# Sinks staged in other buffers, and transposes and products with the values placed later in TensorE's written order: a banded attention with a gated MLP

## Chip, cores, metric

One Trainium2 chip, one core. The metric is the device time of one execution in microseconds (us), the median of several runs. Engines: PE is TensorE (PEld its weight loads), DVE is VectorE, ACT is ScalarE, POOL is GpSimd, SP is SyncE, which issues all DMAs here.

## What is computed

Attention over 4 batches, 8 heads, 768 positions of 64 dimensions; a query sees the first `n_sink` = 4 keys (the sinks) and the last `window` = 128 keys. The result, with the heads side by side (512 columns), goes through an MLP with a short convolution as its gate:

```
scores = scale * q @ k.T           # kept where key < 4 or 0 <= query - key < 128
a   = softmax(scores);  x = a @ v  # x: batch, position, 512
h   = relu(x @ w_in)               # 1024 columns
g   = sigmoid(3-tap convolution of h along the positions)
out = (h * g) @ w_out              # 512 columns
```

All in float32. To keep float32's precision in fast products, most operands are split into a high part and a low part (names with H and L), and three products replace one.

## The kernel before

`banded(c)` (L390) is the path that runs here. Heads are taken in pairs ("groups"): 4 pairs per batch, 16 in all. A pair has 6 tiles of 128 queries, so it takes 6 **steps**; the whole attention has 96 steps, `NSTB` = 24 per batch. Batch 0 (steps 0 to 23) uses plain float32 products and runs beside the loading of the MLP's weights; from batch 1 on keys and queries are split (`A.prep`, L252 to L298).

**What a step does.** The main loop runs over `i`. It writes down, for step `i` and two earlier steps, the parts of the work; each pass has three **slots**, and after each slot come pieces of the MLP (`fill`) and pieces of preparation (`todo`):

- slot 0: `scores(g, t)` (L484) for step `i`: four products into PSUM tiles "sc" (L334, L335), masks and row minimum on DVE (L509, L510), exp on ACT (L513), sum and reciprocal on DVE (L515, L516), normalisation on POOL (L518).
- slot 1: `transp(g, t)` (L527) for step `i - D1` = `i - 1`: two transposes of the weights on PE into "pts" (L548), a copy to SBUF tile "pT" on ACT (L550), two selects on POOL (L552, L554). At every third tile (`u == 2`) the four sink columns of three tiles are gathered: high parts on ACT (L560), low parts on DVE (L561), one transpose of 72 columns on PE (L562, tile "tk"), a copy "sT" on ACT (L564).
- slot 2: `pv(g, t)` (L566) for step `i - D2` = `i - 2`, when a pair's last tile is through: products of the values with pT (L580), five products of the sinks' values `vsr` with sT (L598), and `A.xout`, which splits the result into xH on ACT (L342) and xL on DVE (L343). At a batch's last pair the MLP's next pieces begin here (`cuts`).

The MLP of a batch is spread over the next batch's steps: a unit is 12 products for h (L184, 258 or 260 columns), a chain ACT, DVE, POOL (L191 to L202), and 6 products for the output (L211, 512 columns) in PSUM tiles "po". When 8 units are added up, `second` (L204) copies po to a tile "stm" with tag "st" on ACT (L215) and SP writes it out (L216). "st" has three buffers. The last batch's MLP has no attention beside it.

The preparation of a pair transposes its raw keys and queries in four pieces (`turn_k(0)`, `turn_k(1)`, `turn_q(0)`, `turn_q(1)`): three transposes on PE (L287, L262), two copies on ACT (L290, L250), two subtractions on DVE (L293, L269); after the second piece two DMAs kk<-kk on SP (L297, L298). `coming(n)` says when the pieces are due, as distances in steps. Each piece frees one of four raw buffers, and `fetch()` then issues the next load (L351).

PSUM tag "T" has two buffers. The preparation's transposes, the sinks' transpose and the results px of `pv` (two at a time from batch 1 on) all take theirs from it.

`sink_split` (L376) loads the first four rows of a batch's values to `raw`, splits them to `hi` (ACT, L380) and `lo` (DVE, L381), and issues 18 DMAs that place them in `vsr` (L387). `vsr` exists once. The three tiles have tag "st". The weights come through three buffers of tag "nat" (L97, L100) and are loaded up to step 18.

**What sets the order.** From `i` = `PINNED` = 26 on, PE runs its instructions exactly in the order in which the loop writes them (`c.pin`). Before that, and on all other engines and queues throughout, a planner orders the instructions by its own costs and by their place in the program; each engine then runs its list in order and waits where an operand or a buffer isn't ready.

```
for i in range(NST + D2):
    ...
    for slot in range(SLOTS):
        if slot == 0 and i < NST:
            scores(g, t)
        if slot == 1 and 0 <= i - D1 < NST:
            transp(*steps[i - D1][1:])
        if slot == 2 and 0 <= i - D2 < NST:
            pv(*steps[i - D2][1:])
            ...
        acc += rate / SLOTS
        while acc >= 1.0 and fill:
            fill.pop(0)()
            acc -= 1.0
        while todo and i + (slot + 1) / SLOTS >= todo[0][0]:
            todo.pop(0)[1]()
```

Of the kernel before, what the change touches and what calls it, by code (L numbers as in the profile page):

```python
# [10 lines left out]
F32 = mybir.dt.float32  # L11
F32R = mybir.dt.float32r
# [5 lines left out]
P = 128  # L18
D = 64
NEG = 1.0e9  # L20
NS = 4
SP = 16
SR = 6 * NS
# [15 lines left out]
def f(ap):  # L39
    return ap.bitcast(F32)  # L40
# [334 lines left out]

def sink_split(c, m, vsr, b):  # L376

    raw, hi, lo = (m.mp.tile([P, 512], d, tag="st", name=f"sink{n}{b}", bufs=3)[0:NS] for d, n in ((F32, "r"), (F32R, "h"), (F32R, "l")))
    c.nc.sync.dma_start(raw.rearrange("s (h d) -> s h d", d=D), c.v[b].rearrange("h s d -> s h d")[0:NS])
    c.nc.scalar.copy(hi, raw)  # L380
    c.nc.vector.tensor_tensor(out=lo, in0=raw, in1=f(hi), op=ALU.subtract)  # L381
    for u in range(3):
        for part, val in enumerate((hi, hi, lo)):
            for j in range(2):
                r = SR * part + 2 * NS * u + NS * j
                dst, src = (f(x).rearrange("s (g j d) -> s g j d", j=2, d=D)[:, :, j] for x in (vsr[r:r + NS, u], val))
                c.nc.sync.dma_start(dst, src)  # L387


def banded(c):  # L390

    nc = c.nc
    m = Moe(c)
    A = Attn(c, m.x, KW, m.mp, m.ps)
    T = A.T
    NPAIR = c.H // 2
    NG = c.B * NPAIR
    cp = c.es.enter_context(c.tc.tile_pool(name="bc", bufs=1))
    ap, ps = A.ap, A.ps
# [34 lines left out]
    n0, n1 = T * KW, 3 * NPAIR * P  # L434
# [92 lines left out]
    def transp(g, t):  # L527
        s = st[g]
        hf, u = divmod(t, 3)
        if g < NPAIR:  # L530
            parts = 1 + (t > 0)
            for w in range(parts):
                for j in range(2):
                    c.pin(nc.tensor.transpose(pts[:, w, j, :], s.pe[hf][:, u, j, 0:P] if w else s.pe[hf][:, u, j, KW:SW], c.ident))
            s.pT[t] = ap.tile([P, 2, 2, P], F32, tag="pT", name=f"pT{g}_{t}", bufs=PTB)
            nc.scalar.copy(s.pT[t][:, 0:parts], pts[:, 0:parts])
            if u == 2:
                pk = m.ps.tile([P, P], F32, tag="T", name=f"tk{g}_{t}", bufs=2)
                sk = ap.tile([P, 6, SP], F32, tag="sk", name=f"sk{g}_{hf}")
                nc.scalar.copy(sk, s.pe[hf].rearrange("p t h k -> p (t h) k")[:, :, P:P + SP])  # L540
                c.pin(nc.tensor.transpose(pk[0:6 * SP, :], sk.rearrange("p t k -> p (t k)"), c.ident))
                s.sT[hf] = ap.tile([6 * SP, P], F32, tag="sT", name=f"sT{g}_{hf}")
                nc.scalar.copy(s.sT[hf], pk[0:6 * SP, :])
            return
        pt = pts[:, A.n % 2]
        A.n += 1
        for j in range(2):
            c.pin(nc.tensor.transpose(pt[:, j, :], s.pe[hf][:, u, j, NS:KW], c.ident))  # L548
        own = keytile(g, t)[:, :, 0]
        nc.scalar.copy(own, pt)  # L550
        if t:
            nc.gpsimd.affine_select(out=keytile(g, t - 1)[:, :, 1], in_=own, pattern=[[0, 2], [-1, P]],  # L552
                                    compare_op=ALU.is_gt, fill=c.zero, base=0, channel_multiplier=1)
            nc.gpsimd.affine_select(out=own, in_=own, pattern=[[0, 2], [1, P]], compare_op=ALU.is_ge, fill=c.zero,  # L554
                                    base=0, channel_multiplier=-1)
        if u == 2:
            pk = m.ps.tile([P, P], F32R, tag="T", name=f"tk{g}_{t}", bufs=2)
            sinks = s.pe[hf].rearrange("p t h k -> p (t h) k")[:, :, 0:NS]
            sk = ap.tile([P, 3, 6, NS], F32R, tag="sk", name=f"sk{g}_{hf}")
            nc.scalar.copy(sk[:, 0:3:2], sinks.rearrange("p (o t) k -> p o t k", o=1).to_broadcast([P, 2, 6, NS]))  # L560
            nc.vector.tensor_tensor(out=sk[:, 1], in0=sinks, in1=f(sk[:, 0]), op=ALU.subtract)  # L561
            c.pin(nc.tensor.transpose(pk[0:3 * SR, :], sk.rearrange("p a t k -> p (a t k)"), c.identr))  # L562
            s.sT[hf] = ap.tile([3 * SR, P], F32R, tag="sT", name=f"sT{g}_{hf}")
            nc.scalar.copy(s.sT[hf], f(pk[0:3 * SR, :]))  # L564

    def pv(g, t):  # L566

        s = st[g]
        hp = g % NPAIR
        hf, u = divmod(t, 3)  # L570
        if u < 2 or (g >= NPAIR and hf == 0):
            return
        halves = [hf] if g < NPAIR else [1, 0]
        px = {h: m.ps.tile([P, 3, P], F32, tag="T", name=f"px{g}_{h}", bufs=2).rearrange("p t k -> p (t k)") for h in halves}
        open_ = set()

        def product(j, kt, qt, pT):
            h, at = divmod(qt, 3)
            n = pT.shape[-1]
            c.pin(nc.tensor.matmul(px[h][D * j:D * j + D, P * at:P * at + n], s.v[:, kt, j, :], pT, start=(h not in open_), stop=False,  # L580
                                   skip_group_check=True))

        if g < NPAIR:
            for t1 in range(t, 3 * hf - 1, -1):
                for w in range(1 + (t1 > 0)):
                    for j in range(2):
                        product(j, t1 - w, t1, s.pT[t1][:, w, j, :])
                    open_.add(hf)
        else:
            for kt in range(T - 1, -1, -1):  # L590
                pT = s.pT.pop(kt).rearrange("p h a k -> p h (a k)")
                for lo, hi in [(0, 2 * P)] if kt % 3 < 2 else ([(P, 2 * P)] if kt < T - 1 else []) + [(0, P)]:
                    for j in range(2):
                        product(j, kt, kt + lo // P, pT[:, j, lo:hi])
                    open_.add((kt + lo // P) // 3)
        for h in halves:
            for w in range(1 - h, 3):
                c.pin(nc.tensor.matmul(px[h][:, P * w:P * w + P], (vsr if g >= NPAIR else c.vs)[:, w, P * hp:P * hp + P], s.sT[h],  # L598
                                       start=False, stop=(w == 2), skip_group_check=True))
            A.xout(g, h, px[h])  # L600
# [20 lines left out]
    def coming(n):  # L621

        last = 2 * NPAIR - 2
        if n < last:
            return [(n + 1, -0.4, 1.8)]
        if n == last:
            return [(n + 1, -0.4, 1.4), (n + 2, 1.4, 5.6)]
        return [(n + 2, -0.4 if n > last + 2 else 1.8, 5.1)] if n % 2 == 0 and n + 2 < len(jobs) else []

    for x in prep(0):  # L630
        x()
# [5 lines left out]
    steps = [(n, g, 3 * half + u) for n, (g, half) in enumerate(jobs) for u in range(3)]  # L637
    NST = len(steps)
    NSTB = NPAIR * T
    D1, D2 = 1, 2  # L640
    SLOTS = 3
    fill, todo, after = [], [], None
    rate = acc = 0.0
    cuts = {NSTB // 2: (0, 1, NSTB // 2), NSTB: (1, m.NCH, NSTB)}
    for b in range(1, c.B):
        cuts[NSTB * (b + 1)] = (m.NCH * b, m.NCH * (b + 1), NSTB)

    for i in range(NST + D2):
        if i == PINNED:
            c.pin = c.tc.keep_in_program_order  # L650
        if i < NST:
            n, g, t = steps[i]
            if t % 3 == 0:
                for n1, lo, hi in coming(n):
                    new = prep(n1)
                    todo += [(i + lo + (hi - lo) * (k + 1) / len(new), x) for k, x in enumerate(new)]
            if g >= NPAIR or t % 3 == 2:
                fetch()
            if t == 0 and g and g % NPAIR == 0:
                after = i + 3 if g > NPAIR else i  # L660
            if i == after:
                sink_split(c, m, vsr, g // NPAIR)
            if n + 1 < len(jobs) and (t % 3 == 2 if n < 2 * NPAIR else t == 3):
                values(n + 1)
        if i == NSTB - 3:
            narrow_masks()
        m.need(min(sum(i >= w for w in WHEN), len(m.todo)))
        for slot in range(SLOTS):
            if slot == 0 and i < NST:
                scores(g, t)  # L670
            if slot == 1 and 0 <= i - D1 < NST:
                transp(*steps[i - D1][1:])
            if slot == 2 and 0 <= i - D2 < NST:
                pv(*steps[i - D2][1:])
                if i - D2 + 1 in cuts:
                    while fill:
                        fill.pop(0)()
                    lo, hi, span = cuts[i - D2 + 1]
                    fill = m.pieces(lo, hi)
                    rate = len(fill) / (span - 0.5)  # L680
                    acc = 0.0
            acc += rate / SLOTS
            while acc >= 1.0 and fill:
                fill.pop(0)()
# [3 lines that stand above are left out]
# [145 lines left out]
```

## Time and profile before

| | us |
|---|---|
| median of 3 runs | 523.63 (522.58 to 523.85) |
| the profiled execution | 521.62 |
| its span, first to last instruction | 519.9 |
| PE busy | 462.0 (89%) |
| DVE, ACT, POOL busy | 365.7, 349.1, 288.8 |
| mean granted TensorE clock | 0.975 |

PE's rows overlap: a product's row lasts until its result has drained, while the next has long started. Busy time is the union of the rows. A wait is put down to the last thing that released it.

### The profile page before, as it was taken

Reading aid. Unit: us, or ns where it says so; the run is one execution under the profiler, and the core shown is the slowest. Engines: PE = TensorE matmul, PEld = TensorE weight load, DVE = VectorE, ACT = ScalarE, POOL = GpSimd, SP = SyncE. Lnnn points to the kernel's source line nnn. Section 1 sums busy time; section 2 is a strip of 40 time slices with the busy share of each in tenths; the row PEclk is TensorE's granted clock in tenths of the full one; section 3 lists DMA queues with packets and bytes.
Section 4 is the critical chain, followed back from the end, with each engine's and each line's share of the span. In section 5 each row is a group of like instructions: output and inputs, shape, how many; then the busy total and the mean of one; then the engine's idle time right before and its main releaser. Section 6 shows DMA issues by size and latency. Waiting matters only on the chain.

```text
span 519.9 us, 10426 instructions
## 1 busy us (share of the span) xinstructions
PE 462.0 (89%) x3181; PEld 394.8 (76%) x3181; DVE 365.7 (70%) x1212; ACT 349.1 (67%) x1066; POOL 288.8 (56%) x558
## 2 busy tenths in 40 slices
PE   2787879997988798969999999869999999999995
PEld 2565668886877677858888889757988888899983
DVE  5588899768677666557786978747776976555652
ACT  3887887878676766656776878636776865545452
POOL 3556677545475635555565647445665657254542
PEclk9989989999999998989999999979999999999999
DMA  5867752254323231141323141231312010101011
GB/s 144 219 188 203 206 155 56 65 138 119 76 49 93 72 82 41 40 106 41 94 73 78 44 121 32 59 96 32 92 58 63 1 42 0 43 1 40 5 40 48
DMA packets 87306, 41.02 MB, mean 79 GB/s; under 512 B 80160, under 2 KB 80184, under 8 KB 87240
## 3 DMA queue, kind: packets, MB, share of 16 engines
q1 hardware_dynamic: 87240, 40.25, 29.4%
q8 instruction: 28, 0.46, 0.4%
q14 instruction: 38, 0.31, 0.2%
HBM read 27.60 MB, written 6.29 MB: 65 GB/s over the span
## 4 chain that ended last, share of the span: by engine, by line
PE 47%; DVE 19%; ACT 17%; DMA 5%; POOL 4%; issue 4%; SPq 3%; DVEq 0%; POOLq 0%; ACTq 0%
PE ph L184 16%; PE po L211 13%; PE px L580 5%; DVE t L197 5%; DVE t L196 4%; ACT t L195 3%; ACT hb L191 3%; ACT t L198 2%; SPq L387 2%; PE sc L335 2%; PE sc L334 2%; DVE X L269 2%; PE px L598 2%; PE pts L548 2%; DVE kk L293 2%
## 5 line engine op out<-in xcount | busy, mean ns | idle before, releaser
L211 PE MATMUL po<-woH,g 128*128 128x512 f32 x384 | 148.0, 413 | 11.4 <-ACT stm L215 8.4
L184 PE MATMUL ph<-xH,wiH 128*128 128x258 f32 (+1 forms) x384 | 113.7, 296 | 1.7 <-ACT xH L342 0.9
L184 PE MATMUL ph<-xL,wiH 128*128 128x258 f32 (+1 forms) x384 | 111.2, 290 | 0.4 <-DVE xL L343 0.4
L184 PE MATMUL ph<-xH,wiL 128*128 128x258 f32 (+1 forms) x384 | 111.0, 289 | 0.0
L211 PEld LDWEIGHTS po<-woH,g 128*128 128x128 f32 x384 | 73.2, 192 | 25.4 <-ACT stm L215 9.2
L518 POOL TENSOR_SCALAR pe<-pe,sm 128x132 f32<-128x132 f32 (+1 forms) x144 | 63.6, 453 | 50.7 <-ACT t L195 21.3
L202 POOL TENSOR_TENSOR g<-t,g 128x256 fp32r<-128x256 f32 x96 | 78.5, 817 | 7.2
L184 PEld LDWEIGHTS ph<-xH,wiH 128*128 128x128 f32 x384 | 73.9, 192 | 5.7 <-ACT xH L342 1.6
L211 PE MATMUL po<-woL,g 128*128 128x512 f32 x192 | 77.7, 405 | 0.0
L184 PEld LDWEIGHTS ph<-xH,wiL 128*128 128x128 f32 x384 | 74.2, 193 | 2.4
L184 PEld LDWEIGHTS ph<-xL,wiH 128*128 128x128 f32 x384 | 74.1, 193 | 1.1 <-DVE xL L343 0.9
L198 ACT ACTIVATE t<-t 128x256 f32<-128x256 f32 x96 | 40.2, 418 | 51.7 <-DVE t L197 51.1
L201 POOL TENSOR_SCALAR g<-t 128x256 fp32r<-128x256 f32 x96 | 39.7, 414 | 62.5 <-DVE t L199 45.7
L196 DVE SCALAR_TENSOR_TENSOR t<-hb,cw,t 128x256 f32<-128x256 f32 x96 | 53.4, 556 | 28.3 <-ACT t L195 27.5
L197 DVE SCALAR_TENSOR_TENSOR t<-hb,cw,t 128x256 f32<-128x256 f32 x96 | 57.3, 597 | 6.6
L513 ACT ACTIVATE pe<-pe,sm 128x132 f32<-128x132 f32 (+1 forms) x144 | 57.4, 400 | 5.6 <-DVE sm L510 4.3
L199 DVE SCALAR_TENSOR_TENSOR t<-t,hb 128x256 f32<-128x256 f32 x96 | 44.0, 458 | 23.4 <-ACT t L198 23.1
L552 POOL TENSOR_SCALAR_AFFINE_SELECT pT<-pT 128x256 f32<-128x256 f32 x60 | 27.5, 459 | 58.9 <-ACT pT L550 56.0
L191 ACT ACTIVATE hb<-ph 128x258 f32<-128x258 f32 (+1 forms) x96 | 37.1, 386 | 34.5 <-PE ph L184 33.4
L195 ACT ACTIVATE t<-hb,cw 128x256 f32<-128x256 f32 x96 | 49.0, 510 | 5.7 <-POOL g L202 1.4
L509 DVE COPY_PREDICATED sc<-before,sc 128x128 f32<-128x128 int32 x120 | 31.4, 292 | 21.7 <-PE sc L335 20.8
L580 PE MATMUL px<-pT,vraw 128*64 128x128 f32 (+1 forms) x512 | 43.5, 320 | 0.8 <-DVE kk L293 0.8
(145 smaller groups left out, 964.5 us busy)
## 6 DMA issues: line engine op xcount, KB each, us to landing
raw<-in_q_dram SPq DMA_DIRECT2D x64, 96.0 KB
raw<-in_k_dram SPq DMA_DIRECT2D x64, 96.0 KB
out_dram<-stm SPq DMA_DIRECT2D x24, 256.0 KB
kk<-kk SPq DMA_DIRECT2D x24, 198.0 KB
vraw<-in_v_dram SPq DMA_DIRECT2D x24, 192.0 KB
wi_0r<-in_moe_w_in_dram SPq DMA_DIRECT2D x2, 512.0 KB
wi_1r<-in_moe_w_in_dram SPq DMA_DIRECT2D x2, 512.0 KB
wi_2r<-in_moe_w_in_dram SPq DMA_DIRECT2D x2, 512.0 KB
```

The costliest lines, as they stand in the source:

```text
L184: c.pin(nc.tensor.matmul(u.h[:, 0:W], w[:, cc, ff * P:(ff + 1) * P], x[:, cc, t0:t1], start=(i == 0), stop=(i == len(prods) - 1)))
L191: nc.scalar.activation(hb[:, d0:d0 + W], u.h[:, 0:W], AF.Relu, scale=0.5)
L195: nc.scalar.mul(a, prev, cw[:, 0, ff:ff + 1])
L196: nc.vector.scalar_tensor_tensor(out=e, in0=this, scalar=cw[:, 1, ff:ff + 1], in1=a, op0=ALU.mult, op1=ALU.add)
L197: nc.vector.scalar_tensor_tensor(out=a, in0=nxt, scalar=cw[:, 2, ff:ff + 1], in1=e, op0=ALU.mult, op1=ALU.add)
L198: nc.scalar.activation(e, a, AF.Tanh)
L199: nc.vector.scalar_tensor_tensor(out=a, in0=e, scalar=1.0, in1=this, op0=ALU.add, op1=ALU.mult)
L202: nc.gpsimd.tensor_tensor(out=u.g[:, 1], in0=a, in1=f(u.g[:, 0]), op=ALU.subtract)
L211: c.pin(nc.tensor.matmul(po[:, 0:c.DM], u.g[:, a, tt * P:(tt + 1) * P], w[:, ff, :], start=(ff == 0 and i == 0), stop=(ff == NFF - 1 and i ...
L513: nc.scalar.activation(pe[:, j, cols], pe[:, j, cols], AF.Exp, bias=sm[:, j:j + 1], scale=-1.0, accum_out=sm[:, 2 + 2 * j:3 + 2 * j])
L518: nc.gpsimd.tensor_scalar(pe[:, j, cols], pe[:, j, cols], sm[:, 8 + j:9 + j], 1.0, ALU.mult, ALU.mult)
L580: c.pin(nc.tensor.matmul(px[h][D * j:D * j + D, P * at:P * at + n], s.v[:, kt, j, :], pT, start=(h not in open_), stop=False, skip_group_c ...
```

## The change

The split's three tiles move from tag "st" to tag "nat". From batch 1 on, the sinks' transpose becomes a function of its own, `transp_sinks`, in slot 0 of two steps after the tile (behind that step's scores), while the gathering on ACT and DVE stays in `transp`; `transp` itself moves from slot 1 to slot 2; `pv` moves from slot 2 of `i - 2` to slot 1 of `i - 3`. Batch 0 stays as it was. The pieces of preparation get fixed places: at 1, 2, 4 and 5 steps from the pair's start (before: 0.98, 2.35, 3.73, 5.10, and for the first such pair 2.63, 3.45, 4.28, 5.10). The second stretch of MLP pieces is spread over one step more.

```
 def sink_split(c, m, vsr, b):
-    raw, hi, lo = (m.mp.tile([P, 512], d, tag="st", name=f"sink{n}{b}", bufs=3)[0:NS] for d, n in ((F32, "r"), (F32R, "h"), (F32R, "l")))
+    raw, hi, lo = (m.mp.tile([P, 512, 2], d, tag="nat", name=f"sink{n}{b}", bufs=3).rearrange("p n w -> p (n w)")[0:NS, 0:512]
+                   for d, n in ((F32, "r"), (F32R, "h"), (F32R, "l")))
...
         if u == 2:
-            pk = m.ps.tile([P, P], F32R, tag="T", name=f"tk{g}_{t}", bufs=2)
             sinks = s.pe[hf].rearrange("p t h k -> p (t h) k")[:, :, 0:NS]
-            sk = ap.tile([P, 3, 6, NS], F32R, tag="sk", name=f"sk{g}_{hf}")
+            sk = s.sk = ap.tile([P, 3, 6, NS], F32R, tag="sk", name=f"sk{g}_{hf}")
...
-            c.pin(nc.tensor.transpose(pk[0:3 * SR, :], sk.rearrange("p a t k -> p (a t k)"), c.identr))
-            s.sT[hf] = ap.tile([3 * SR, P], F32R, tag="sT", name=f"sT{g}_{hf}")
-            nc.scalar.copy(s.sT[hf], f(pk[0:3 * SR, :]))
+
+    def transp_sinks(g, t):
+        s = st[g]
+        hf, u = divmod(t, 3)
+        if g < NPAIR or u < 2:
+            return
+        pk = m.ps.tile([P, P], F32R, tag="T", name=f"tk{g}_{t}", bufs=2)
+        c.pin(nc.tensor.transpose(pk[0:3 * SR, :], s.sk.rearrange("p a t k -> p (a t k)"), c.identr))
+        s.sT[hf] = ap.tile([3 * SR, P], F32R, tag="sT", name=f"sT{g}_{hf}")
+        nc.scalar.copy(s.sT[hf], f(pk[0:3 * SR, :]))
...
-            return [(n + 1, -0.4, 1.8)]
+            return [(n + 1, None, -0.4, 1.8)]
         if n == last:
-            return [(n + 1, -0.4, 1.4), (n + 2, 1.4, 5.6)]
-        return [(n + 2, -0.4 if n > last + 2 else 1.8, 5.1)] if n % 2 == 0 and n + 2 < len(jobs) else []
+            return [(n + 1, None, -0.4, 1.4), (n + 2, None, 1.4, 5.6)]
+        return [(n + 2, (1.0, 2.0, 4.0, 5.0))] if n % 2 == 0 and n + 2 < len(jobs) else []
...
-    D1, D2 = 1, 2
+    D1, D2, DL = 1, 2, 3
...
-    cuts = {NSTB // 2: (0, 1, NSTB // 2), NSTB: (1, m.NCH, NSTB)}
+    cuts = {NSTB // 2: (0, 1, NSTB // 2), NSTB: (1, m.NCH, NSTB + 1)}
...
-            if slot == 1 and 0 <= i - D1 < NST:
+            if slot == 0 and 0 <= i - D2 < NST:
+                transp_sinks(*steps[i - D2][1:])
+            if slot == (1 if i - D1 < NSTB else 2) and 0 <= i - D1 < NST:
                 transp(*steps[i - D1][1:])
-            if slot == 2 and 0 <= i - D2 < NST:
-                pv(*steps[i - D2][1:])
...
+            for d, at in ((D2, 2), (DL, 1)):
+                if slot == at and 0 <= i - d < NST and (i - d < NSTB) == (d == D2):
+                    pv(*steps[i - d][1:])
...
```

## Rows read from the trace of the kernel before

**Rows 1.** The page's first part: busy time of each engine, its share of the span, and the number of instructions.
```profile
PE 462.0 (89%) x3181; PEld 394.8 (76%) x3181; DVE 365.7 (70%) x1212; ACT 349.1 (67%) x1066; POOL 288.8 (56%) x558
```

**Rows 2.** Busy time of each engine in four stretches: attention of batches 1, 2 and 3, cut at the first score product of each, and a piece of the last batch's MLP. Columns: the stretch, its length, then PE, PEld, DVE, ACT, POOL busy (with instructions), granted clock, DMA share, GB/s.
```profile
105.90:206.60 100.70, 87.55 (x616) 73.90 (x616) 69.68 (x280) 71.38 (x234) 52.93 (x119) 0.97 0.34 85
206.60:320.40 113.80, 106.61 (x760) 93.00 (x759) 83.71 (x304) 80.26 (x259) 67.43 (x142) 0.99 0.29 72
320.40:435.00 114.60, 106.78 (x759) 93.46 (x757) 83.65 (x300) 77.28 (x251) 68.38 (x142) 0.97 0.20 50
448.00:510.00 62.00, 62.00 (x393) 55.84 (x392) 36.72 (x66) 30.82 (x71) 30.23 (x44) 1.00 0.07 27
```

**Rows 3.** Columns as in rows 2, for the four stretches of these batches in which the granted clock was at the lower level.
```profile
179.80:183.20 3.40, 3.33 (x13) 2.85 (x14) 0.20 (x1) 1.46 (x5) 2.53 (x6) 0.50 0.00 0
196.80:200.20 3.40, 3.40 (x14) 2.80 (x13) 1.40 (x5) 1.86 (x4) 0.87 (x2) 0.50 0.11 26
231.00:234.40 3.40, 3.40 (x16) 3.21 (x15) 0.24 (x1) 0.00 (x0) 0.07 (x1) 0.51 0.94 260
343.60:350.40 6.80, 4.07 (x16) 3.79 (x17) 0.77 (x2) 0.92 (x2) 1.68 (x4) 0.50 0.52 138
```

**Rows 4.** Who PE waited for over the whole span: the waiting instruction, what released it, us in total, times, the longest.
```profile
PE tk L562 <- DVE sk L561: 11.1, 15, 1.6
PE po L211 <- ACT stm L215: 8.4, 2, 4.7
...
PE pts L548 <- POOL pe L518: 6.6, 8, 2.6
```

**Rows 5.** PE in order of time behind batch 3's output copy: start, duration, instruction, and in brackets the idle time before it and its releaser.
```profile
346.33 0.80 PE L211 MATMUL po<-woH,g 128*128 128x512 f32 x1 [4.69 <-ACT stm L215]
...
350.64 0.28 PE L184 MATMUL ph<-xH,wiL 128*128 128x258 f32 x1
350.76 0.28 PE L184 MATMUL ph<-xL,wiH 128*128 128x258 f32 x1
```

**Rows 6.** SP's DMA issues in order of time for batch 2's sinks: the load, a later load of keys, and the first two and the last of the writes' rows.
```profile
170.47 0.34 SPq L379 DMA_DIRECT2D sinkr<-in_v_dram  x1
...
210.67 0.90 SPq L351 DMA_DIRECT2D raw<-in_k_dram  x2
...
215.12 2.86 SPq L387 DMA_DIRECT2D vsr<-sinkh  x4
218.09 1.32 SPq L387 DMA_DIRECT2D vsr<-sinkl  x2
...
228.80 1.32 SPq L387 DMA_DIRECT2D vsr<-sinkl  x2
```

**Rows 7.** ACT in order of time in the same stretch: the second output copy.
```profile
229.97 0.58 ACT L215 COPY stm<-po 128x512 f32<-128x512 f32 x1 [0.81 <-DMA vsr<-sinkh]
```

**Rows 8.** All engines in order of time around one sinks' transpose in batch 1; the first and the last row are a step's last score product and its normalisation.
```profile
140.90 0.28 PE L335 MATMUL sc<-kk,X 128*128 128x260 f32 x1
...
142.57 0.21 ACT L560 CAST sk<-pe 128x48 fp32r<-128x48 f32 x1
143.51 0.32 DVE L561 TENSOR_TENSOR sk<-pe,sk 128x24 fp32r<-128x24 f32 x1
...
143.88 0.25 PE L562 MATMUL tk<-identr,sk 128*72 128x128 f32 x1 [1.26 <-DVE sk L561]
...
144.48 0.98 POOL L518 TENSOR_SCALAR pe<-pe,sm 128x132 f32<-128x132 f32 x2
```

**Rows 9.** Columns as in rows 2, for single pairs, six steps each: one of batch 1 and one of batch 2 without a sinks' split beside them.
```profile
128.10:152.50 24.40, 22.04 (x160) 18.66 (x159) 17.28 (x70) 17.20 (x58) 14.60 (x33) 1.00 0.29 67
...
237.80:264.70 26.90, 26.28 (x194) 23.08 (x193) 21.04 (x77) 19.02 (x64) 17.19 (x34) 1.00 0.24 57
```

**Rows 10.** All engines in order of time at the longest wait of the transposes, with batch 2's split on ACT and DVE.
```profile
175.65 0.60 ACT L380 CAST sinkh<-sinkr 4x512 fp32r<-4x512 f32 x1
...
177.36 0.82 DVE L381 TENSOR_TENSOR sinkl<-sinkr,sinkh 4x512 fp32r<-4x512 f32 x1
...
179.31 0.33 PE L548 MATMUL pts<-ident,pe 128*128 128x128 f32 x1 [2.64 <-POOL pe L518]
```

**Rows 11.** All engines in order of time at a piece of preparation of the keys with MLP work beside it: the transposes, and the subtractions that free the PSUM buffer.
```profile
367.98 0.49 PE L287 MATMUL tk<-ident,raw 128*128 128x128 f32 x3
...
369.39 1.14 DVE L293 TENSOR_TENSOR kk<-tk,kk 64x384 fp32r<-64x384 f32 x2 [0.18 <-ACT kk L290]
```

**Rows 12.** All engines in order of time where a product with the values waited: the keys' transposes, the products of one half, the subtractions that free the PSUM buffer, the products of the other half.
```profile
323.95 0.49 PE L287 MATMUL tk<-ident,raw 128*128 128x128 f32 x3
...
325.76 1.52 PE L580 MATMUL px<-pT,vraw 128*64 128x128 f32 x16
...
326.79 1.14 DVE L293 TENSOR_TENSOR kk<-tk,kk 64x384 fp32r<-64x384 f32 x2
...
328.07 1.30 PE L580 MATMUL px<-pT,vraw 128*64 128x128 f32 x12 [0.79 <-DVE kk L293]
```

More of the change, by code (lines that the diff above doesn't have):

```diff
@@ L643, in banded @@
     rate = acc = 0.0
-    cuts = {NSTB // 2: (0, 1, NSTB // 2), NSTB: (1, m.NCH, NSTB)}
+    cuts = {NSTB // 2: (0, 1, NSTB // 2), NSTB: (1, m.NCH, NSTB + 1)}
     for b in range(1, c.B):
         cuts[NSTB * (b + 1)] = (m.NCH * b, m.NCH * (b + 1), NSTB)
-    for i in range(NST + D2):
+    for i in range(NST + DL):
         if i == PINNED:
@@ L653, in banded @@
             if t % 3 == 0:
-                for n1, lo, hi in coming(n):
+                for n1, at, *ends in coming(n):
                     new = prep(n1)
-                    todo += [(i + lo + (hi - lo) * (k + 1) / len(new), x) for k, x in enumerate(new)]
+                    if at is None:
+                        at = [ends[0] + (ends[1] - ends[0]) * (k + 1) / len(new) for k in range(len(new))]
+                    todo += [(i + w, x) for w, x in zip(at, new)]
             if g >= NPAIR or t % 3 == 2:
@@ L670, in banded @@
                 scores(g, t)
-            if slot == 1 and 0 <= i - D1 < NST:
+            if slot == 0 and 0 <= i - D2 < NST:
+                transp_sinks(*steps[i - D2][1:])
+            if slot == (1 if i - D1 < NSTB else 2) and 0 <= i - D1 < NST:
                 transp(*steps[i - D1][1:])
-            if slot == 2 and 0 <= i - D2 < NST:
-                pv(*steps[i - D2][1:])
[L675 to L681, printed above, removed]
+            for d, at in ((D2, 2), (DL, 1)):
+                if slot == at and 0 <= i - d < NST and (i - d < NSTB) == (d == D2):
+                    pv(*steps[i - d][1:])
+                    if i - d + 1 in cuts:
+                        while fill:
+                            fill.pop(0)()
+                        lo, hi, span = cuts[i - d + 1]
+                        fill = m.pieces(lo, hi)
+                        rate = len(fill) / (span - 0.5)
+                        acc = 0.0
             acc += rate / SLOTS
```

## The prediction

> **What bounds the kernel now.** I read the engines' shares first. PE is busy 462.0 us of the 519.9 us span, 89%; no other engine is over 70% [rows 1]. Next, the stretches cut at the first score product of each batch: 105.9 us is where batch 1's attention starts, 206.6 batch 2's, 320.4 batch 3's, and from about 435 us the last batch's MLP runs alone. In that last stretch PE is busy 62.00 of 62.00 us: nothing there can be gained by order. In the three attention stretches PE is idle 13.15, 7.19 and 7.82 us, 28.2 us together [rows 2], and in four stretches it runs at a granted clock of 0.50, the lower of its two levels (1.2 GHz), each right behind a stall; they hold 14.20 us of PE work, half of which, 7.1 us, is the price [rows 3]. So 35.3 us can come out of these stretches by waits alone, and the other engines, at most 74% busy in any of them, don't forbid it.
>
> Then the list of waits says which. PE waited 11.1 us in 15 waits for the sinks' transpose's operand (DVE L561), 8.4 us in 2 waits for the output copy (ACT L215), 6.6 us in 8 waits for the normalised weights (POOL L518) [rows 4]. These three are 26.1 of the 28.2 us, and the change touches each. A removed wait gives a little more than its idle time: busy products start 0.12 us apart though each row lasts 0.28 (350.64 to 350.76 [rows 5]), so a product before a stall hides 0.16 us of drain less.
>
> **The change, part by part.** The sum is made against the profiled execution, 521.62 us (span 519.9 and 1.7 around it); the median of the runs, 523.63, lies 2.0 above it. The work of every engine stays; only order and buffers change.
>
> 1. *Sinks in the weights' staging.* The split holds all three "st" buffers. In batch 2 its load was issued at 170.47, but its 18 writes to vsr only from 215.12 to 230.1, since vsr is read until the previous batch's last products; 6 writes to a row pair take 4.2 us of SP's time [rows 6]. The MLP's second output copy, at 229.97, waited for a buffer of these writes [rows 7], and PE for that copy: 4.69 us in batch 3 [rows 5], 8.4 together. The weights' buffers are idle after step 18, so nothing waits for them. Gain: 8.4, 2 x 0.16, and the low clock that follows each stall, 3.40 and 4.07 us of work at half rate, so 1.7 and 2.0 [rows 3]: **12.4 us**. Nothing is late next: the other output copies cost PE no wait. The clock I take from rows; the Trainium skill (TensorE: Matmul & The Clock Gate, Terms) takes the throttled time times the missing share of the clock, which over all four stretches gives 8.5 us where I count 7.1; the sum would be 1.4 larger by it. The trace differs because 2.8 of those 17.0 us were idle.
>
> 2. *Sinks' transpose one slot and a step boundary later.* Its operand goes POOL, ACT (142.57), DVE (143.51 to 143.83), PE at 143.88 [rows 8]: DVE started 0.73 us after ACT ended, with other work before it. Now at least the rest of a slot's MLP and the next scores lie between. A slot is a third of a step: 24.4 us for six steps is 1.36 [rows 9], and without stalls (100.70 less 13.15 idle less 3.37 for the clock, over 24 steps) 1.17. Only the longest wait, 1.6, exceeds that. Gain 11.1 + 15 x 0.16 = 13.5, less 0.6 left: **12.9 us**. Its ACT copy and the five products that read it stay far apart: both moved by two slots.
>
> 3. *Transposes one slot later.* From the last score product to the normalised weights it takes 141.18 to 145.46, 4.3 us [rows 8]; four slots of 1.17 less the scores' 0.5 are 4.2, five are 5.4. So typical waits go. The 2.64 us at 179.31 stands behind the split's own 0.60 on ACT and 0.82 on DVE [rows 10]; these now run elsewhere, but I leave it half. Gain 6.6 + 8 x 0.16 = 7.9, less 2.0 left, and of the 3.33 and 3.40 us at low clock around them [rows 3] 2.4 of the 3.4 us: **8.3 us**. The pT copy and both selects on POOL move with the transposes; the products behind them got two slots later, so their distance grows by one.
>
> 4. *Products with the values two slots later, preparation at 1, 2, 4, 5.* This adds a wait. The products need both of the two PSUM buffers "T" (tag of the preparation and of px). The keys' second half is now transposed one slot before them (it was three slots for the first half). The buffer is free when DVE has made the low part: 369.39 + 1.14 against transposes over at 368.47, 2.1 us, or 324.44 to 327.93, 3.5 us [rows 11, 12]. Cover: one slot (1.17 in batch 1, 26.9/18 = 1.49 later [rows 9]) and the products of the other half, 1.52 [rows 12]: 2.7 and 3.0; 2.0 at a batch's cut, where the MLP's pieces have run out. Before, such a wait occurred once, 0.79 at 328.07 [rows 12]. Ends: nothing, and 3.5 us in all ten groups, 3 x 0.8 + 5 x 0.5 + 2 x 1.5 = 7.9. Nearer are the short evictions: 0.4 for three groups of batch 1, 0.1 for five, 1.0 at the two cuts, less the 0.8 of now: **-2.9 us**. Behind a waiting product on PE stand all its later products; DVE, ACT and POOL then catch up, so it is paid once. The two kk copies on SP and the loads that follow a freed raw buffer move earlier with the preparation; a load has a whole pair ahead of it.
>
> 5. *Batch 1's pace.* PE would ask 3.51 us a step instead of 4.20. ACT was busy 71.38 of 100.70 us [rows 2], 85% at the new pace, so queues grow. From nothing to 0.2 us a step; I take 0.1: **-2.4 us**.
>
> 6. *The seam at steps 24 and 25.* Keys of the second pair are prepared before batch 0's last products, whose sinks lie in the same kk buffer, so one T buffer is held through it. PE had other work there; between 0 and 2 us, I take **-0.5**. The changed cut spreads batch 0's MLP over one more step: no cost, it fills the tail before the cut.
>
> Sum: 12.4 + 12.9 + 8.3 - 2.9 - 2.4 - 0.5 = 27.8 us; 521.62 - 27.8 = 493.8 as profiled, **495.8 us** as a median. With every stall gone it would be 12.4 + 13.5 + 11.3 + 0.8 = 38.0 less, 485.6.
>
> **The rivals.** (a) *The two PSUM buffers become the wait*: item 4 at its far end (-7.9) and item 5 at 0.2 a step (-4.8) give a gain of 20.4, 503.2 us. For it: one slot of cover against 3.5 us. Against: only one eviction in the rows was that long, in a stretch without MLP work.
> (b) *The sinks' bubble stays*: it repeats every third step, and if a buffer is behind it a later place moves it to whoever comes next. Then items 1 and 3 alone count: 12.4 + 8.3 - 2.4 - 0.5 = 17.8, 505.8 us. Against: the wait ended on DVE L561, an operand, each time [rows 4]. The Trainium skill (Perfetto Trace Analysis, Optimization Strategy) says that a gap which repeats can mean too few SBUF or PSUM buffers; that rule speaks for (b), and this trace speaks against it.
> (c) *Slower: SP's queue stands*. The split no longer waits for "st", so it can be queued earlier, and if its 18 writes come before the loads in SP's order, SP stands until the previous batch's last products. Now loads stand between (one at 210.67 [rows 6]). The point is where SP stands longer than the raw buffers last, one pair of 24.4 us: 215.12 - 170.47 = 44.7 would starve PE by some 20 us in each of two batches, 40 - 27.8 = 12 slower, 536 us. Only a queue ordered by something other than readiness does that.
> (d) *It does not do what it says*: the softmax chain's 4.3 us, not the order, sets the pace, and waits return elsewhere: 523.6. Against: PE idles 0.6 us in a group of 26.9 without a split [rows 9].
>
> **How the numbers follow.** Forecast 0.62 (487 to 500), (a) 0.19, (b) 0.08, (c) 0.06, (d) 0.04; 0.01 for more gain than the sum without stalls. A measurement here tells 0.3%, 1.6 us, from no change. Faster 0.90 (forecast, (a), (b)), same 0.04, slower 0.06. The range takes the forecast's own lower end and reaches over (a): 487 to 505.
>
> **What would show it.** Right: no PE wait for L215, low clock stretches after 231 us gone; the sinks' transpose waits under 1 us in sum; waits on L518 under 3 us, in batch 1 only; six steps of batch 1 in 21 to 22.5 us; a few waits of px on DVE L293, mostly at cuts. Wrong: px waits over 6 us (a); waits on L561 as many as now (b); loads issued behind vsr writes and scores waiting for kk (c); batch 1 at 24 us per six steps (item 5).

## The result, and the profile after

The changed kernel takes **500.75 us** (median of 4 runs, 499.88 to 501.28) against 523.73 for the kernel before in the same comparison: a ratio of 0.9564 [0.9545, 0.9583], 23.0 us less. The forecast was 495.8 with 487 to 505 as its range. Its profiled execution took 501.28 us (span 499.2), where the sum had come to 493.8: 7.5 us of the forecast 27.8 did not come. Two executions of the third set of experiments, at 1531 and 1878 us, are left out of all medians below.

From line 379 on, lines are one further than before; after the new function they are seven further. The page's first part, to be read beside [rows 1]:

```profile
PE 456.6 (91%) x3181; PEld 393.2 (79%) x3181; DVE 366.6 (73%) x1212; ACT 348.7 (70%) x1066; POOL 287.2 (58%) x558
```

The stretches of batches 1, 2 and 3, cut as in [rows 2] (the third ends where the last step's work has drained), and the whole of them up to the first score product of step 95:

```profile
106.40:195.60 89.20, 80.25 (x601) 69.27 (x600) 69.33 (x271) 68.25 (x226) 50.90 (x115) 1.00 0.39 95
195.60:304.20 108.60, 105.62 (x758) 92.52 (x757) 86.03 (x310) 80.99 (x262) 65.52 (x140) 1.00 0.30 75
304.20:412.00 107.80, 105.73 (x763) 93.22 (x762) 82.17 (x298) 75.87 (x249) 68.00 (x143) 1.00 0.21 53
...
106.40:407.30 300.90, 286.90 (x2085) 250.60 (x2084) 233.98 (x865) 222.98 (x728) 180.69 (x389) 1.00 0.30 75
```

The same whole stretch in the kernel before:

```profile
105.90:429.90 324.00, 295.84 (x2098) 255.89 (x2098) 233.33 (x869) 225.31 (x732) 184.15 (x391) 0.97 0.28 69
```

These two rows are the account. The stretch is 23.1 us shorter. PE's idle time fell from 28.2 to 14.0, so 14.2 us came out of waits; PE's busy time fell by 8.9, of which 7.1 is the low clock, gone from every one of these stretches (granted clock 1.00). The stretch also holds 21 fewer of the MLP's products of L184: the start has 8 more and the tail 12 more, and the start is 0.5 us longer, the tail 1.9 (90.0 to 91.9). So 23.1 - 1.9 - 0.5 = 20.7, the difference of the spans.

Who PE waits for now, against [rows 4] (us in total, times, the longest):

```profile
PE pts L549 <- POOL pe L519: 6.8, 10, 1.6
...
PE tk L287 <- ACT pT L551: 2.1, 1, 2.1
PE px L587 <- DVE kk L293: 2.0, 6, 0.5
PE sc L334 <- PE sc L335: 1.7, 2, 0.9
...
PE tk L287 <- ACT sT L544: 0.7, 1, 0.7
```

Two of the three large rows of before are gone: no wait for the sinks' low parts and none for the output copy. The third, the transposes' wait for the normalised weights, is as large as it was (6.6, 8 times). New are two waits at steps 24 and 25 (tk L287) and two of the scores; px waits for a PSUM buffer six times, where it did once (0.8 us). The profile puts the scores' two waits down to PE itself, but both end 0.1 us behind DVE's second row minimum of a pair's last tile (scores at 150.70 and 196.83, minima over at 150.60 and 196.73).

**Where the ten waits stand.** Nine of ten are of a pair's last tile (t = 5); four of the ten, 2.4 us, are in batches 2 and 3. DVE, POOL and PE in the trace after, around the last tile of batch 2's second pair; its last score product ends at 245.16:

```profile
244.96 0.30 DVE L510 COPY_PREDICATED sc<-before,sc 128x128 f32<-128x128 int32 x1
245.16 1.02 DVE L196 SCALAR_TENSOR_TENSOR t<-hb,cw,t 128x256 f32<-128x256 f32 x1
...
246.31 0.28 DVE L511 CUSTOM_DVE_ANT_0 pe<-sc,m 128x132 f32<-128x132 f32 x1
...
247.09 1.14 DVE L269 SCALAR_TENSOR_TENSOR X<-tq,X 64x384 fp32r<-64x384 f32 x2
248.26 0.30 DVE L511 CUSTOM_DVE_ANT_0 pe<-sc,m 128x132 f32<-128x132 f32 x1
...
251.00 0.54 POOL L519 TENSOR_SCALAR pe<-pe,sm 128x132 f32<-128x132 f32 x1
...
251.60 0.33 PE L549 MATMUL pts<-ident,pe 128*128 128x128 f32 x1 [0.70 <-POOL pe L519]
```

The same tile in the kernel before; its last score product ends at 261.44:

```profile
262.02 0.29 DVE L510 CUSTOM_DVE_ANT_0 pe<-sc,m 128x132 f32<-128x132 f32 x1
262.23 0.08 DVE L510 DVE_READ_ACCUMULATOR2_ANT sm<- 128x1 f32 x1
262.23 0.29 DVE L510 CUSTOM_DVE_ANT_0 pe<-sc,m 128x132 f32<-128x132 f32 x1
...
265.39 1.14 DVE L269 SCALAR_TENSOR_TENSOR X<-tq,X 64x384 fp32r<-64x384 f32 x2
```

The two subtractions of the queries' last piece (L269; the same 1.14 us in both) stood behind this tile's row minima. Now the piece comes at 5.0 instead of 5.10, one slot earlier, ahead of the tile's scores, and the subtractions stand between its two minima: the second minimum is through 3.4 us after the last score product (248.56) where it took 1.1 (262.52), and the normalised weights come after 6.4 us instead of 4.1.

### The profile page after: what moved, and what is told of

Same layout as the page of the kernel before. It is cut to its first block, busy times and chain, and to the rows that moved or that the text cites. A ratio compares the mean times of both kernels' runs of the same rounds, so it can differ in the third digit from the quotient of the medians.

```text
span 499.2 us, 10421 instructions
## 1 busy us (share of the span) xinstructions
PE 456.6 (91%) x3181; PEld 393.2 (79%) x3181; DVE 366.6 (73%) x1212; ACT 348.7 (70%) x1066; POOL 287.2 (58%) x558
## 4 chain that ended last, share of the span: by engine, by line
PE 54%; DVE 21%; ACT 11%; POOL 6%; issue 3%; DMA 3%; SPq 1%; POOLq 0%; DVEq 0%; ACTq 0%
PE ph L184 17%; PE po L211 16%; PE px L587 5%; DVE t L197 4%; DVE t L196 4%; PE pts L549 3%; ACT t L195 3%; PE sc L331 2%; PE px L605 2%; PE sc L335 2%; PE sc L334 2%; DVE X L269 2%; ACT t L198 2%; ACT hb L191 2%; ACT pe L514 2%
## 5 line engine op out<-in xcount | busy, mean ns | idle before, releaser
L211 PE MATMUL po<-woH,g 128*128 128x512 f32 x384 | 145.0, 407 | 3.0 <-POOL g L201 2.6
L184 PE MATMUL ph<-xL,wiH 128*128 128x258 f32 (+1 forms) x384 | 112.6, 293 | 0.7 <-DVE xL L343 0.6
L184 PE MATMUL ph<-xH,wiH 128*128 128x258 f32 (+1 forms) x384 | 111.3, 290 | 0.3 <-ACT xH L342 0.2
L184 PE MATMUL ph<-xH,wiL 128*128 128x258 f32 (+1 forms) x384 | 110.6, 288 | 0.0
L201 POOL TENSOR_SCALAR g<-t 128x256 fp32r<-128x256 f32 x96 | 39.9, 416 | 84.6 <-DVE t L199 71.0
L211 PEld LDWEIGHTS po<-woH,g 128*128 128x128 f32 x384 | 72.2, 189 | 16.5 <-POOL g L201 3.4
L202 POOL TENSOR_TENSOR g<-t,g 128x256 fp32r<-128x256 f32 x96 | 79.2, 825 | 4.9
L519 POOL TENSOR_SCALAR pe<-pe,sm 128x132 f32<-128x132 f32 (+1 forms) x144 | 63.4, 452 | 30.6 <-DVE sm L517 17.4
L184 PEld LDWEIGHTS ph<-xH,wiH 128*128 128x128 f32 x384 | 73.4, 191 | 4.2 <-ACT xH L342 0.7
L211 PE MATMUL po<-woL,g 128*128 128x512 f32 x192 | 76.1, 396 | 0.0
L184 PEld LDWEIGHTS ph<-xH,wiL 128*128 128x128 f32 x384 | 73.3, 191 | 2.5
L196 DVE SCALAR_TENSOR_TENSOR t<-hb,cw,t 128x256 f32<-128x256 f32 x96 | 52.7, 549 | 30.4 <-ACT t L195 29.5
L184 PEld LDWEIGHTS ph<-xL,wiH 128*128 128x128 f32 x384 | 73.7, 192 | 1.3 <-DVE xL L343 1.1
L199 DVE SCALAR_TENSOR_TENSOR t<-t,hb 128x256 f32<-128x256 f32 x96 | 44.7, 466 | 20.4 <-ACT t L198 19.7
L587 PE MATMUL px<-pT,vraw 128*64 128x128 f32 (+1 forms) x512 | 45.5, 323 | 2.3 <-DVE kk L293 2.0
L191 ACT ACTIVATE hb<-ph 128x258 f32<-128x258 f32 (+1 forms) x96 | 36.9, 384 | 8.6 <-PE ph L184 6.4
L334 PE MATMUL sc<-kk,X 128*128 128x260 f32 (+1 forms) x144 | 41.0, 305 | 2.0 <-PE sc L335 1.7
L510 DVE COPY_PREDICATED sc<-before,sc 128x128 f32<-128x128 int32 x120 | 31.7, 291 | 13.9 <-PE sc L335 12.9
```

The costliest lines, as they stand in the source:

```text
L184: c.pin(nc.tensor.matmul(u.h[:, 0:W], w[:, cc, ff * P:(ff + 1) * P], x[:, cc, t0:t1], start=(i == 0), stop=(i == len(prods) - 1)))
L191: nc.scalar.activation(hb[:, d0:d0 + W], u.h[:, 0:W], AF.Relu, scale=0.5)
L196: nc.vector.scalar_tensor_tensor(out=e, in0=this, scalar=cw[:, 1, ff:ff + 1], in1=a, op0=ALU.mult, op1=ALU.add)
L202: nc.gpsimd.tensor_tensor(out=u.g[:, 1], in0=a, in1=f(u.g[:, 0]), op=ALU.subtract)
L211: c.pin(nc.tensor.matmul(po[:, 0:c.DM], u.g[:, a, tt * P:(tt + 1) * P], w[:, ff, :], start=(ff == 0 and i == 0), stop=(ff == NFF - 1 and i ...
L334: self.c.pin(self.nc.tensor.matmul(pc, X[:, j, u, :], kk[:, j, lo:hi], start=True, stop=False))
```

## The experiments

Twelve kernels. Differences are against the median of the changed kernel, 500.75 us, or of the kernel before, which took 523.48, 523.44 and 523.16 us in the three sets.

**1. The staging alone.** The kernel before with the split's tiles in "nat" and nothing else:

```
-    raw, hi, lo = (m.mp.tile([P, 512], d, tag="st", ...
+    raw, hi, lo = (m.mp.tile([P, 512, 2], d, tag="nat", ...
```

> The kernel before with only the sinks' split moved to the weights' buffers (tag nat). Theory (item 1 of the prediction): the two waits of the output copy (8.4 us of PE) and the low clock behind each (3.7 us) go, 12.4 us: about 511.3 us, and no PE wait on the output copy L215 is left. Rival: the stall only moves, because SP still needs some 12 us for the 18 writes and other things stand behind them: over 520 us.

515.34 us, ratio 0.9859 [0.9793, 0.9925]: 8.1 less, not 12.4. Waits in this kernel:

```profile
PE tk L563 <- DVE sk L562: 10.7, 16, 1.6
PE pts L549 <- POOL pe L519: 10.0, 12, 2.5
```

The wait for the copy is gone, but the transposes' waits rose from 6.6 to 10.0, so part of the gain is given back at once. The two largest new ones, 2.51 us and 1.4 us, come at steps 54 and 78, where the copy's waits of before had come at steps 52 and 76. At the first, the low part of the next sinks' split stands in front of the queries' subtractions and the tile's sum on DVE, and 6.80 us at the lower clock follow:

```profile
228.32 0.68 DVE L382 TENSOR_TENSOR sinkl<-sinkr,sinkh 4x512 fp32r<-4x512 f32 x1 [1.75 <-ACT X L250]
...
232.30 0.99 PE L549 MATMUL pts<-ident,pe 128*128 128x128 f32 x2 [2.51 <-POOL pe L519]
```

```profile
232.00:238.80 6.80, 6.10 (x21) 4.93 (x21) 1.98 (x7) 1.82 (x7) 4.66 (x10) 0.50 0.00 1
```

So here the split, earlier by now, makes part of the new wait itself; that the stalls removed had also given the softmax time fits the second place, but no run here separates the two.

**2. The sinks' transpose alone.** The kernel before with `transp_sinks` in slot 0 of `i - 2`:

```
+            if slot == 0 and 0 <= i - D2 < NST:
+                transp_sinks(*steps[i - D2][1:])
```

> The kernel before with only the sinks' transpose moved to slot 0 of two steps after its tile; its gathering, the transposes, the products with the values, the preparation and the staging stay. Theory (item 2): the 11.1 us of waits on the low parts of the sinks go to under 1 us, 12.9 us: about 510.8 us. Rival (b): a buffer of tag T or the softmax chain is behind it, the waits move to the transposes or to px, and the time stays at 520 us or more.

514.22 us, ratio 0.9832 [0.9767, 0.9896]: 9.3 less, not 12.9. Its waits:

```profile
PE po L211 <- ACT stm L215: 9.5, 2, 5.2
PE pts L548 <- POOL pe L518: 8.8, 7, 2.9
```

No wait for L561 is left, with the same PSUM buffers: rival (b) falls. Again the other waits rose, the copy's from 8.4 to 9.5 and the transposes' to 8.8, and the lower clock took 9.0 us of batches 1 to 3 where it had taken 7.1.

**3. All but the staging.** The changed kernel with the split back in "st":

> The changed kernel (500.8 us) with the sinks' split back in the three buffers of the outputs (tag st). Theory: the two waits on the output copy and the low clock behind them come back, 12.4 us: about 513 us. Rival: the later places alone already let the output copies pass (other order on ACT and SP), and it stays within 3 us of 500.8.

509.3 us, ratio 0.9737 [0.9674, 0.9799]: 8.5 lost. The wait for the output copy is back, at 4.0 us where it was 8.4 before. Three stretches of 3.4 us at the lower clock come with it; one of them, at 334.2, stands behind the copy's wait, the others behind a wait of the preparation (115.1) and one of the transposes (176.8), so that only 1.7 of the 5.0 us that they cost is tied to it:

```profile
PE po L211 <- ACT stm L215: 4.0, 2, 2.0
```

The edit is worth 8.1 alone and 8.5 as the last one, both under the 12.4 of the sum.

**4. The queries' last piece back at 5.1.**

```
-        return [(n + 2, (1.0, 2.0, 4.0, 5.0))] if ...
+        return [(n + 2, (1.0, 2.0, 4.0, 5.1))] if ...
```

> The changed kernel with one number changed: the queries' second half is prepared at 5.1 steps instead of 5.0, that is one slot later, behind the scores of the pair's last tile instead of ahead of them. Theory: at 5.0 its two subtractions on DVE (1.14 us) and two copies on ACT stand in front of that tile's row minimum, stretch its softmax chain from 4.3 to 5.4 to 6.5 us, and cause the 6.8 us of waits of the transposes on the normalisation that are left, and the 2.0 us of waits of the next scores. At 5.1 these waits fall under 2 us together: 492 to 495 us. Rival: the pace of DVE, ACT and POOL sets it, and the waits stay or go to another tile: 499 to 502 us.

497.33 us, ratio 0.9503 [0.9442, 0.9564]: 3.4 less. The scores' waits fell from 1.7 to 0.2 us, those of the transposes only from 6.8 to 5.8. In the profiles PE's idle time in batches 1 to 3 is 2.8 us less (11.2 against 14.0), but one stretch at the lower clock takes 1.7 back, so these batches are only 1.6 us shorter (299.3 against 300.9). Batch 0, where PE's order is the same in both, is 1.4 shorter, so the size of the edit's own gain is uncertain. Batch 1 in this kernel, the same piece:

```profile
146.51 0.29 DVE L511 CUSTOM_DVE_ANT_0 pe<-sc,m 128x132 f32<-128x132 f32 x1
...
147.22 1.14 DVE L269 SCALAR_TENSOR_TENSOR X<-tq,X 64x384 fp32r<-64x384 f32 x2 [0.41 <-ACT X L250]
...
149.28 0.15 DVE L516 TENSOR_REDUCE sm<-sm 128x2 f32<-128x4 f32 x1
```

The subtractions now stand behind both minima, but still ahead of the tile's sum (L516), inside the same chain. Half of the theory held.

**5. Both query pieces earlier,** at 3.5 and 4.5 in place of 4.0 and 5.0:

> The changed kernel with the queries' two halves prepared one slot earlier each (3.5 and 4.5 instead of 4 and 5). Theory: the second half's subtractions (1.14 us of DVE) then stand a slot further ahead of the last tile's scores and its chain gets shorter than at 5.0 and at 5.1 (where they stood behind its scores but still ahead of its sum): waits of the transposes on the normalisation 2 to 4 us, waits of the scores on each other gone, 495 to 498 us. Rival: they now stretch the chain of the tile before, and the sum of waits stays at 6 us or more: 500 us.

510.2 us, ratio 0.9745 [0.971, 0.978]: 9.5 us worse. The theory missed, and its rival held: all seven waits are now of the tile before the last (t = 4). Waits and DVE's rows in batch 1:

```profile
PE pts L549 <- POOL pe L519: 10.3, 7, 2.7
```

```profile
148.34 0.30 DVE L510 COPY_PREDICATED sc<-before,sc 128x128 f32<-128x128 int32 x1 [0.58 <-PE sc L335]
148.67 1.12 DVE L269 SCALAR_TENSOR_TENSOR X<-tq,X 64x384 fp32r<-64x384 f32 x2
149.82 0.30 DVE L510 COPY_PREDICATED sc<-before,sc 128x128 f32<-128x128 int32 x1
...
151.37 0.29 DVE L510 COPY_PREDICATED sc<-before,sc 128x128 f32<-128x128 int32 x1
151.77 1.14 DVE L269 SCALAR_TENSOR_TENSOR X<-tq,X 64x384 fp32r<-64x384 f32 x2
152.95 0.30 DVE L510 COPY_PREDICATED sc<-before,sc 128x128 f32<-128x128 int32 x1
...
153.37 0.15 DVE L516 TENSOR_REDUCE sm<-sm 128x2 f32<-128x4 f32 x1
```

The first piece falls between the two masks (L510) of t = 4 and the second between those of t = 5; but the sum of t = 4 (L516 at 153.37) comes behind both, so both are in its chain. The expectation had followed PE's order; what decided was where 1.14 us landed in DVE's list. In the profile the stretch of batches 1 to 3 lost 9.8 us: 3.7 more idle time and 6.7 for the lower clock, less 0.6 elsewhere. Three of its four low stretches stand behind these waits.

**6. The seam's pieces at their old places** (1.8 to 5.1 for the first pair):

> The changed kernel (500.8 us) with the old places of the preparation for the first pair alone, whose keys are prepared at steps 26 and 27 instead of 24 and 25. Theory: at steps 24 and 25 the keys' transposes waited 0.7 and 2.1 us for a PSUM buffer of tag T (held until batch 0's last products are through); with the old places these go, 3 us: about 498 us. Rival: the wait belongs to the seam between the planner's order and the written one, and stays in another form (before, 0.8 us of it was there): 500 to 501 us.

500.82 us, ratio 0.9571 [0.9536, 0.9606]: no gain. The 2.8 us of waits at steps 24 and 25 went. Smaller ones came (px 0.7, the queries' transposes 0.4, pts 0.4 more), and PE's idle time in batches 1 to 3 fell from 14.0 to 12.5 us; but one stretch at the lower clock, from 175.8 to 179.2, cost 1.7. It stands behind a wait of 1.55 us that the changed kernel has too (1.56 at 176.43), without such a stretch.

**7. The transposes behind slot 2's MLP pieces** instead of ahead of them:

```
-            if slot == (1 if i - D1 < NSTB else 2) and 0 <= i - D1 < NST:
+            if slot == 1 and 0 <= i - D1 < min(NST, NSTB):
                 transp(*steps[i - D1][1:])
...
+            if slot == 2 and NSTB <= i - D1 < NST:
+                transp(*steps[i - D1][1:])
             while todo and ...
```

> The changed kernel with the transposes behind the MLP's pieces of their slot instead of ahead of them, nothing else. That gives the softmax chain 0.6 us (batch 1) to 1.0 us more. Theory: what is left of the transposes' waits (6.8 us in 10 waits, nearly all on a pair's last tile) is a chain of 5.4 to 6.5 us against a cover of 5.0 to 5.5; with the longer cover under 2.5 us are left: 495 to 497 us. Rival: DVE, ACT and POOL set the pace, the chain grows with the cover and the waits stay at 5 us or more: 499 to 502 us.

**495.24 us**, ratio 0.9461 [0.943, 0.9492]: 5.5 less than the changed kernel, the fastest version here. Waits and the whole stretch:

```profile
PE px L587 <- DVE kk L293: 3.7, 7, 0.9
PE pts L549 <- POOL pe L519: 3.6, 5, 1.1
```

```profile
105.00:400.60 295.60, 284.24 (x2086) 250.15 (x2084) 234.33 (x865) 223.71 (x727) 183.21 (x388) 1.00 0.30 76
```

More cover halves the transposes' waits; px gives 1.7 us of it back.

**8. Experiments 5, 6 and 7 together:**

> The changed kernel with all three: the first pair's preparation at its old places, the transposes behind the MLP's pieces, and the queries' halves one slot earlier. If each theory holds: waits on the normalisation under 1.5 us, seam gone, 491 to 494 us. If the pace of the other engines is the limit: 497 us or more.

507.46 us, ratio 0.9686 [0.9632, 0.974]: the early pieces outweigh the cover. The output products wait more for the MLP's own chain, 3.7 us for L201 and 3.2 for L202 (2.6 and 0.3 in the changed kernel), and two stretches at the lower clock cost 3.4.

**9. Experiments 4 and 7 together:**

> The changed kernel with the transposes behind the MLP pieces of slot 2 and the queries' last piece back at 5.1, the two single edits that gave 495.2 and 497.3 us. Theory (two different waits: cover for the transposes, and the place of two subtractions on DVE): they add in part, waits on the normalised weights (L519) under 2 us in sum, no wait on L334, 492 to 494 us. Rival (both remove the same waits of a pair's last tile): no further gain, 495 us or more.

497.23 us, ratio 0.9517 [0.9486, 0.9548]. The rival's time held: no further gain, and 2.0 us more than experiment 7 alone. The two edits remove the same waits in the main, but more are left than with the cover alone (4.7 against 3.6), and px now waits most:

```profile
PE px L587 <- DVE kk L293: 5.0, 8, 1.2
...
PE pts L549 <- POOL pe L519: 4.7, 5, 1.5
```

**10. The transposes back in slot 1,** all else changed (item 3 undone alone):

```
-            if slot == (1 if i - D1 < NSTB else 2) and 0 <= i - D1 < NST:
+            if slot == 1 and 0 <= i - D1 < NST:
```

> The changed kernel with the two transposes back in slot 1 in every batch, all else as changed: undoes item 3 alone. Prediction's item 3: 8.3 us are lost, 509 us. Theory after the trace (the later slot hides all but a pair's last tile): waits on L519 rise from 6.8 us in 10 to over 12 us in at least 20, with stretches at the lower clock behind them, 507 to 512 us. Rival (only the clock part came from the later slot): waits on L519 stay near 7 us, some low clock, about 503 us.

505.36 us, ratio 0.9662 [0.9637, 0.9688]: 4.6 lost, between theory and rival. Waits, and the transposes' group over batches 1 to 3 (count, busy us, mean ns, idle before):

```profile
PE pts L549 <- POOL pe L519: 9.1, 17, 1.4
```

```profile
L549 PE MATMUL pts<-ident,pe 128*128 128x128 f32 x140 | 33.5, 292 | 9.9 <-POOL pe L519 9.1
```

and the whole stretch of batches 1 to 3:

```profile
105.50:411.40 305.90, 292.17 (x2086) 251.38 (x2084) 233.82 (x865) 223.18 (x728) 180.28 (x391) 0.99 0.29 73
```

The transposes' group in the changed kernel:

```profile
L549 PE MATMUL pts<-ident,pe 128*128 128x128 f32 x140 | 29.8, 281 | 7.0 <-POOL pe L519 6.8
```

The later slot takes out 2.9 us of idle time and 3.7 us of the transposes' own busy rows (a wait between a tile's two transposes leaves each to drain alone: they stand 0.2 us or more apart in 27 tiles of 72 here, in 10 of the changed kernel). One stretch at the lower clock, 1.6 us, goes too, but it stands behind the seam's wait (tk L287, 2.1 us), which both kernels have, so it is not shown to be the slot's. Against it px waits 2.0 us here and 0.2 without the later slot, and the scores 1.2 more.

**11 and 12. The same 1.14 us on DVE, in two places.** The subtractions of one piece are done twice, the same values being written again; in 11 those of the second piece, as here, in 12 those of the first (`half == 0`):

```
-            for j in range(2):
+            for j in (0, 1, 0, 1)[0:4 if half == 1 else 2]:
                 nc.vector.scalar_tensor_tensor(out=X[rows[1 - j], j], ...
```

> The changed kernel with the two DVE subtractions of the queries' second piece (turn_q(1), L269) done twice, 1.14 us more on DVE once in each of the 12 pairs prepared this way (the same values are written again). Theory (they stand inside the chain of a pair's last tile, which PE already waits for): nearly each of these waits grows, L519 from 6.8 to 12 to 16 us in sum, low clock stretches in batch 1, 507 to 513 us. Rival (DVE at 73% has room, what counts is its sum): under 2 us, as in the run that doubles the first piece.

> The changed kernel with the two DVE subtractions of the queries' first piece (turn_q(0)) done twice: the same 1.14 us on DVE once in each of 12 pairs, but one step earlier, behind the row minimum of a tile whose chain takes 3.4 us against a cover of 5. Theory (the place counts): waits on L519 rise by under 3 us, 500 to 504 us. Rival (the sum on DVE counts): as much as when the second piece is doubled.

Second piece doubled: 516.31 us, ratio 0.9886 [0.9843, 0.993], 15.6 lost. First piece doubled: 508.48 us, ratio 0.972 [0.967, 0.9769], 7.7 lost. The waits of 11, then those of 12:

```profile
PE pts L549 <- POOL pe L519: 15.1, 13, 2.8
...
PE px L587 <- DVE kk L293: 3.8, 6, 1.4
```

```profile
PE pts L549 <- POOL pe L519: 7.0, 15, 1.6
...
PE po L211 <- POOL g L201: 3.7, 4, 2.0
...
PE po L211 <- POOL g L202: 1.6, 3, 0.8
```

The transposes' waits came out as the theory said: 8.3 us more in 11, 0.2 more in 12. In 11, twelve of the thirteen waits are of t = 5. So the second piece is in the chain that PE waits for, and place counts, since the same work costs 15.6 us there and 7.7 one step earlier. But the first piece is in a chain too, that of t = 4, and the 0.2 hides an exchange: in 12 the waits of t = 4 rose from 0.3 to 3.5 us and those of t = 5 fell from 6.5 to 3.5. Both times were above the theory. In 12 PE also waits 2.4 us more for the MLP's chain (DVE L196 to L199, then POOL L201 and L202), and three stretches ran at the lower clock, half of whose PE time, 4.9 us, is lost (in 11 two stretches, 3.4 us):

```profile
114.10:117.50 3.40, 3.00 (x14) 3.03 (x15) 2.23 (x10) 1.55 (x6) 0.00 (x0) 0.50 0.58 161
151.70:155.10 3.40, 3.35 (x11) 2.20 (x10) 2.35 (x10) 2.06 (x10) 2.79 (x7) 0.50 0.00 0
179.00:182.40 3.40, 3.40 (x17) 3.38 (x17) 2.36 (x10) 2.45 (x9) 1.94 (x6) 0.50 0.25 58
```

Without the clock's part, the stretch of batches 1 to 3 is 12.7 us longer in 11 (317.0 - 300.9 - 3.4) and 4.1 in 12 (309.9 - 300.9 - 4.9).

## Why the prediction came out as it did, point by point

1. **Staging, 12.4.** Its mechanism was right: in the changed kernel the waits and the low clock behind them are gone. Alone it gave 8.1 and as the last edit 8.5, so the term was 4 us too large. What failed in it is "Nothing is late next": in experiment 1 the transposes' waits rise by 3.4 us, most of it two steps behind where the copy's had been, with the split itself in front of one, and the lower clock still costs 3.1 there. As the last edit it had only 4.0 us of the copy's wait left to remove.

2. **Sinks' transpose, 12.9.** Right in its mechanism: 11.1 us of waits fell to none, 0.6 better than forecast; alone it gave 9.3 us of time, since other waits and the lower clock took more (experiment 2). Its drain was small: the group's busy time fell by 1.0 us (6.1 to 5.1 for 23 transposes), not 15 x 0.16 = 2.4. This gap, which repeated every third step, was an operand's, and a later place removed it without another buffer (experiment 2). The Trainium skill (Perfetto Trace Analysis, Optimization Strategy) names too few SBUF or PSUM buffers as what a gap that repeats can mean; this trace does not agree, by the 11.1 us that went.

3. **Transposes, 8.3: the step that failed.** I forecast 2.0 us of their waits left, in batch 1 only; 6.8 were, 2.4 of them in batches 2 and 3, and only the clock came as forecast (all 3.4 us, where I had counted 2.4). Two things are behind it. First, 6.6 was the wrong number to start from: with other stalls removed these waits are 10.0, 8.8 and, with all else changed, 9.1 (experiments 1, 2, 10). Item 5 had held 2.4 us for such a thing, about this difference, as a pace and not as a wait on L519. Second, five slots do cover a usual chain, but a pair's last tile has a longer one, since the preparation's last piece was moved ahead of its scores by the same change. The prediction costed that move for the keys' PSUM buffer alone (item 4) and left out the queries' evictions on ACT and DVE. Experiment 11 shows that they stand in the chain PE waits for; experiments 4 and 7, which move them or add cover, give 3.4 and 5.5 us back in the medians, 1.6 and 5.3 in the profiled stretch of batches 1 to 3.

4. **px on the keys' eviction, -2.9.** Right: 2.0 us in 6 waits, and 1.4 more in px's busy rows. Rival (a) did not come. Experiment 10 adds that these waits go with the transposes' later slot (0.2 without it).

5. **Batch 1's pace, -2.4.** Six steps took 21.5 to 23.3 us, where 21 to 22.5 was to show it right; the waits of the scores (1.7) are new, and they too end behind the last tile's minima.

6. **The seam, -0.5.** 2.8 us of waits, more than the 2.0 of its far end. But putting the pieces back gained nothing in the medians (experiment 6): 1.5 us less idle time and 1.7 us more for the lower clock, so what the seam costs stays open.

In the profiles: 6.4 us are short in item 3 (a forecast gain of 5.9 beside the clock's, against waits 0.2 and busy rows 0.3 larger than before), 2.3 in item 6, 0.8 in item 2, about 0.6 in item 5 (an estimate from the rows of L334: 1.9 more idle and 1.1 more busy, less the 2.4); the clock of item 3 gave 1.0 more, and a wait on L191 of 0.8 went. That makes 8.3 where 7.5 us are missing, so the account closes within 1 us. In medians only 5.0 are missing, since the profiled run before lay 2.0 under its median and that after 0.5 over it. Rivals (c) and (d) did not come: the writes to vsr begin at 208.03, behind the loads as before, and scores wait for no keys.

## What to carry to other kernels

Removing one wait can lengthen the next one on the same chain: read the wait that a later edit meets from a kernel that has the earlier edits (alone, two edits gave 8.1 of 12.4 and 9.3 of 12.9 here). When a piece of work is moved, follow its evictions in the lists of DVE and ACT and ask which tile's chain they now stand in; the order written for TensorE does not tell. Where an operand was late here, the cheapest remedy was cover, and the cheapest cover was to put the consumer behind work that is in the same slot already (experiment 7).

## What was not expected of the hardware

The same 1.14 us of DVE work, twelve times, costs 15.6 us in one place and 7.7 in another, though DVE is busy only 73% of the span; 12 x 1.14 = 13.7 lies between. A wait's idle time is not its whole price: in experiment 10 the idle time of the whole stretch is as in the changed kernel (305.9 - 292.17 = 13.7 against 14.0), and the loss is in PE's busy rows. And the lower clock came and went with waits of one or two microseconds in batch 1: none in the changed kernel and in experiment 7, three stretches of 3.40 us in experiment 12. The same wait of 2.1 us (tk L287, at 114 to 117 us) is followed by such a stretch in experiments 5, 10, 11 and 12 and by none in the changed kernel and in experiments 4, 7 and 9. Which of such waits is followed by one was not settled, and each stretch of 3.40 us can cost up to 1.7.
